# Reordering LayerNorm transposes, attention and the first stage in a two-layer transformer kernel

## The chip, the cores and the metric

The kernel runs on one core of one Trainium2 chip. The metric is device time in microseconds (us) for one execution; I quote the median of several runs. The kernel before takes 1357.69 us (median of 5 runs, 1355.87 to 1361.27).

Short names, as the profile has them: PE is TensorE (matmul), DVE is VectorE, ACT is ScalarE, POOL is GpSimd, SP is SyncE (here it only starts DMA transfers).

## The reference

Two layers. Each is a dilated sliding-window attention block followed by a feed-forward block, both with LayerNorm in front and a residual.

```python
# S=2048 rows, D=1024, H=32 heads of 32, window W=8 with dilation 2, F=3584; bf16
def A(x, wqkv, wo):                   # attention
    q, k, v = split(x @ wqkv)         # 1024 -> 3 * 1024
    logits = q . k[pos - 2*w] * 32**-0.5,  w = 0..7     # masked where pos < 2*w
    o = sum_w softmax(logits)[w] * v[pos - 2*w]
    return o @ wo
def B(x, w1, b1, w2, b2):             # feed-forward
    return gelu(x @ w1 + b1) @ w2 + b2
for layer in range(2):
    x = x + A(layernorm(x), wqkv, wo)
    x = x + B(layernorm(x), w1, b1, w2, b2)
```

## The kernel before

The 2048 rows are cut into four blocks of 512. Two layers of four blocks make eight **stages**, 0 to 7. The attention of a stage depends only on its own rows and a halo of 14 rows, so the stages are pipelined: while PE does the feed-forward block of stage n, it also projects Q, K, V for stage n+3, and DVE computes attention.

The framework places every instruction on its engine **in a fixed order at compile time**, from program order, priorities and a model of the times. In the traces each engine follows that order: DVE's evictions that were ready at 482.7 us start at 492.24 us, after the multiply that stands before them (shown below).

LayerNorm: arithmetic on DVE, the reciprocal root on POOL, then the transposes on PE, all for one tile of 128 rows at a time.

```python
def ln_T(xt, xnT, c):
    st = ...; nc.vector.bn_stats(...) x2; nc.vector.bn_aggr(mv, st)
    nc.vector.tensor_scalar(ve, mv[:, 1:2], EPS, None, ALU.add)
    nc.gpsimd.tensor_tensor(rs, ve, mhalf, ALU.pow)               # POOL: 1/sqrt
    nc.vector.tensor_scalar(xn, xt, mv[:, 0:1], rs, ALU.subtract, ALU.mult)
    for k in range(KT):                                           # 8 transposes on PE
        nc.tensor.transpose(pt[:, k, :], xn[:, k * P:(k + 1) * P], ident)
    nc.scalar.copy(xnT[:, :, c * P:(c + 1) * P], pt)
# LN1 (before the projections) and WO (before the feed-forward block) call ln_T for c = 0..3
```

Attention (about 81 us of DVE per stage) is traced with the lowest priority, right after its projections. Its largest steps are multiplies over 128 x 8192 elements.

```python
def ATT(l, j):
    # loads q, k, v from the scratch that QKV wrote
    with tc.high_priority(offset=-LOWP):
        # halos; per pair of window positions: pr = q * k (128 x 8192), three adds ("qk groups")
        # softmax; the exponential is on ACT
        # per pair: pr = v * aw (128 x 8192), adds into o ("value part")
    # stores o to scratch
```

Output projection and second feed-forward matmul. There are six PSUM accumulators for all matmuls; W2 holds four of them until DVE has added them to the residual ("eviction").

```python
def WO(l, j):
    # oT <- one load; two weight chunks
    for c in range(NC):
        for hf in range(2):
            # 8 matmuls into ps;  DVE: xr += ps
        ln_T(xr, xn2T, c)                 # LayerNorm 2 with its transposes, inside the loop
        nc.vector.tensor_tensor(xr, xr, b2bc, ALU.add)
def W2(l, j, hf):
    # 4 accumulators; weights in 4 groups of 7
    for g in range(4):
        for kk in range(7):
            for c in range(NC):
                nc.tensor.matmul(accs[c], ...)
    for c in range(NC):
        nc.vector.tensor_tensor(sl, accs[c], sl, ALU.add)
```

The order of the whole (shortened like the code above; the whole kernel follows):

```python
    LN1(0); QKV(0, mid=LN1(1)); att(0)    # "mid": LN1 of the next stage at weight chunk 2
    QKV(1, mid=LN1(2)); att(1)
    QKV(2, mid=LN1(3)); att(2)
    QKV(3, chunks 0..3); WO(0); QKV(3, chunks 4..5); att(3)
    for n in range(8):
        W1(n, mid=LN1(n + 3));            # n + 3 only where 1 <= n and n + 3 < 8
        QKV(n + 3); att(n + 3)
        W2(n, first half); WO(n + 1); W2(n, second half)
```

## Time and profile before

| | before |
|---|---|
| median of 5 runs | 1357.69 us |
| span of the profiled run | 1355.3 us |
| PE busy | 1272.8 us |
| matmuls / transposes on PE | 5632 / 512 |

The page's part on busy time (busy us, share of the span, number of instructions):

```profile
PE 1272.8 (94%) x6144; PEld 585.5 (43%) x6144; DVE 861.7 (64%) x831; ACT 352.8 (26%) x500; POOL 305.9 (23%) x346
```

PE is the engine that bounds the kernel, but a busy PE is not a fast PE. The timeline of PE (start us, duration us, engine, line, instruction, count; in brackets the idle time before it and what ended it) shows this in two places:

```profile
458.34 24.34 PE L316 MATMUL psw<-wchunk,h 128*128 128x512 bf16 x112
482.51 3.62 PE L275 MATMUL pswo<-wchunk,oT 128*128 128x512 bf16 x16
492.97 9.09 PE L275 MATMUL pswo<-wchunk,oT 128*128 128x512 bf16 x28 [6.84 <-DVE xr L322]
...
1139.71 48.51 PE L298 MATMUL psw<-xn2T,wchunk 128*128 128x512 bf16 x224
1188.06 24.34 PE L316 MATMUL psw<-wchunk,h 128*128 128x512 bf16 x112
```

From 1139.71 to 1188.06 us nothing waits: 224 matmuls in 48.35 us, 0.2159 us each. At 492.97 us PE has waited 6.84 us for an eviction, and the next 28 matmuls take 9.09 us where 28 x 0.2159 = 6.05 would do, so a wait costs more than its length: the granted clock is 0.50 from 492.97 to 497 us. DVE's timeline at the same moment says why the eviction was late:

```profile
487.89 4.42 DVE L223 TENSOR_TENSOR pr<-q,k 128x8192 bf16<-128x8192 bf16 x1
492.24 2.48 DVE L322 TENSOR_TENSOR xr<-psw,xr 128x512 bf16<-128x512 f32 x4
494.63 1.28 DVE L280 TENSOR_TENSOR xr<-pswo,xr 128x512 bf16<-128x512 f32 x2
```

W2's matmuls had been done by 482.7 us, but their four evictions (L322) stand in DVE's order behind attention, the last of it a 4.42 us multiply.

The waits of PE (in total us, times, longest us):

```profile
PE ptr L134 <- DVE xn L131: 26.7, 26, 6.2
PE pswo L275 <- DVE xr L322: 22.8, 5, 8.1
PE ptr L134 <- DVE ve L127: 12.6, 5, 6.7
PE ptr L134 <- POOL rs L129: 12.5, 1, 12.5
```

Three of the four are transposes (ptr) waiting for LayerNorm; the last one is the start.

The table of windows gives each stage (window in us; busy us of each engine; the granted PE clock; DMA share; GB/s):

```profile
core 0: us, PE busy (x) PEld busy (x) DVE busy (x) ACT busy (x) POOL busy (x), PEclk, DMA share, GB/s
356.48:533.17 176.69, 161.60 (x769) 73.84 (x768) 158.00 (x134) 45.61 (x64) 38.10 (x46) 0.95 0.70 214
698.98:862.27 163.29, 157.07 (x770) 71.75 (x769) 106.00 (x105) 44.94 (x63) 43.63 (x46) 1.00 0.69 213
1139.71:1253.16 113.45, 112.82 (x546) 51.61 (x545) 21.52 (x41) 23.30 (x32) 22.51 (x29) 1.00 0.50 167
```

The three rows are stages 1, 3 and 6 (a stage is counted from the first matmul of its W1). I call **loss** the length of a window minus 0.2159 us for each of its matmuls and 0.0556 us for each transpose (8 take about 0.45). Stages 1 and 3 hold the same work, 704 matmuls and 64 transposes, 155.5 us: they lose 21.2 and 7.8. Stage 6 loses 1.2. Over the whole span the work is 1244.1 us and the loss 111.2.

### The profile page before, as it was taken

The page shows a single profiled execution, that of the slowest core. Times are in us where ns is not written, and L with a number is a line of the kernel's source. Part 1 is how long each engine was busy: PE and PEld are TensorE (multiplying, and loading weights), DVE is VectorE, ACT ScalarE, POOL GpSimd, SP SyncE. Part 2 cuts the span into 40 slices and gives each one's busy share as a digit, 9 for nine tenths or more (in the row PEclk, how much of TensorE's full clock was granted, in tenths as well). Part 3 has the DMA queues.
Part 4 walks back from the last instruction along what each step waited for, and adds up shares of the span by engine and source line. Part 5 has one row for each costly group of instructions (what it writes and reads, how often), then busy time and mean ns, then how long its engine had stood idle before and what let it go on. Part 6 is the DMA issues. An engine that isn't in the chain of part 4 may idle for free.

```text
span 1355.3 us, 14546 instructions
## 1 busy us (share of the span) xinstructions
PE 1272.8 (94%) x6144; PEld 585.5 (43%) x6144; DVE 861.7 (64%) x831; ACT 352.8 (26%) x500; POOL 305.9 (23%) x346
## 2 busy tenths in 40 slices
PE   5899898997989979999899998999999999999998
PEld 3344344443444434444344444444444444444443
DVE  4379999999899989912999049970599451023001
ACT  2334223411234102432024311243113301401310
POOL 4312021111321212412133121322232122111110
PEclk9899899998989989999999999999999999999999
DMA  8665484773775947569575695756947437544542
GB/s 249 209 140 125 89 252 155 215 226 118 229 218 175 291 122 240 185 207 276 149 235 191 212 280 155 246 186 220 265 139 232 171 127 239 184 147 148 183 136 86
DMA packets 76866, 259.17 MB, mean 191 GB/s; under 512 B 8832, under 2 KB 17024, under 8 KB 74752
## 3 DMA queue, kind: packets, MB, share of 16 engines
q0 software_dynamic: 56352, 212.88, 49.6%
q1 hardware_dynamic: 16704, 45.09, 12.2%
q8 instruction: 48, 0.79, 0.3%
q10 hardware_dynamic: 3744, 0.27, 0.2%
q14 instruction: 18, 0.15, 0.0%
HBM read 216.28 MB, written 41.94 MB: 191 GB/s over the span
## 4 chain that ended last, share of the span: by engine, by line
PE 46%; DVE 35%; DMA 10%; issue 5%; POOL 4%; ACT 0%; SPq 0%; POOLq 0%; DVEq 0%
PE psw L298 18%; PE psqkv L171 12%; PE psw L316 12%; DVE pr L223 6%; DVE pr L247 4%; DVE pr L226 4%; DVE bnst L123 3%; POOL rs L129 3%; DMA k<-scrK 3%; PE pswo L275 2%; DVE pr L227 2%; DMA scrK<-stage 2%; DMA xin<-in_A_x_dram 2%; DMA v<-scrV 2%; DVE xn L131 2%
## 5 line engine op out<-in xcount | busy, mean ns | idle before, releaser
L298 PE MATMUL psw<-xn2T,wchunk 128*128 128x512 bf16 x1792 | 392.8, 381 | 0.7 <-DVE xr L322 0.7
L316 PE MATMUL psw<-wchunk,h 128*128 128x512 bf16 x1792 | 391.2, 379 | 0.0
L171 PE MATMUL psqkv<-xnT,wchunk 128*128 128x512 bf16 x1536 | 339.3, 383 | 1.1 <-ACT xnT L135 1.1
L298 PEld LDWEIGHTS <-wchunk 128*128 128x128 bf16 x1792 | 175.5, 98 | 210.6 <-issue 3.9
L316 PEld LDWEIGHTS <-h 128*128 128x128 bf16 x1792 | 174.8, 98 | 208.6
L171 PEld LDWEIGHTS <-wchunk 128*128 128x128 bf16 x1536 | 151.5, 99 | 183.7 <-issue 7.6
L303 ACT ACTIVATE h<-psw,b1raw 128x512 bf16<-128x512 f32 x224 | 154.0, 687 | 282.3 <-PE psw L298 282.2
L117 POOL DMA_DIRECT2D wchunk<-in_B_w_dram x120 | 114.6, 955 | 468.8 <-PE psw L316 208.8
L322 DVE TENSOR_TENSOR xr<-psw,xr 128x512 bf16<-128x512 f32 x64 | 39.5, 680 | 236.0 <-PE psw L316 236.0
L178 ACT CAST stage<-psqkv 128x512 bf16<-128x512 f32 x192 | 112.3, 586 | 210.1 <-PE psqkv L171 209.7
L275 PE MATMUL pswo<-wchunk,oT 128*128 128x512 bf16 x512 | 123.0, 396 | 22.8 <-DVE xr L322 22.8
L223 DVE TENSOR_TENSOR pr<-q,k 128x8192 bf16<-128x8192 bf16 x32 | 141.6, 4424 | 0.9
L247 DVE TENSOR_TENSOR pr<-v,aw 128x8192 bf16<-128x8192 bf16 x32 | 141.5, 4421 | 0.8
L210 DVE COPY k<-k 32x448 bf16<-32x448 bf16 x24 | 6.4, 268 | 183.0 <-DMA k<-scrK 182.7
L135 ACT COPY xn2T<-ptr 128x1024 bf16<-128x1024 bf16 x32 | 32.4, 1012 | 334.5 <-PE ptr L134 334.5
L129 POOL TENSOR_TENSOR rs<-ve,mhalf 128x1 f32<-128x1 f32 x64 | 62.3, 978 | 202.7 <-DVE ve L127 197.1
L134 PE MATMUL ptr<-ident,xn 128*128 128x128 bf16 x512 | 44.2, 240 | 52.7 <-DVE xn L131 26.7
L275 PEld LDWEIGHTS <-oT 128*128 128x128 bf16 x512 | 51.1, 101 | 85.4 <-issue 34.0
L226 DVE TENSOR_TENSOR pr<-pr 128x4096 bf16<-128x4096 bf16 x32 | 73.0, 2283 | 0.7
L134 PEld LDWEIGHTS <-xn 128*128 128x128 bf16 x512 | 34.9, 108 | 75.6 <-DVE xn L131 66.6
L123 DVE BATCH_NORM_STATS2 bnst<-xin 128x6 f32<-128x512 bf16 x64 | 41.2, 669 | 34.7 <-DMA xin<-in_A_x_dram 27.8
L117 POOL DMA_DIRECT2D wchunk<-in_A_wqkv_dram x30 | 26.9, 897 | 142.0 <-PE psw L298 93.6
(51 smaller groups left out, 608.5 us busy)
## 6 DMA issues: line engine op xcount, KB each, us to landing
wchunk<-in_B_w_dram POOLq DMA_DIRECT2D x56, 1024.0 KB, 6.3
wchunk<-in_B_w_dram POOLq DMA_DIRECT2D x64, 896.0 KB, 6.3
wchunk<-in_A_wqkv_dram POOLq DMA_DIRECT2D x30, 1024.0 KB, 6.3
wchunk<-in_A_wo_dram POOLq DMA_DIRECT2D x16, 1024.0 KB, 8.5
scrQ<-stage POOLq DMA_DIRECT2D x8, 1024.0 KB, 8.8
q<-scrQ SPq DMA_DIRECT2D x8, 1024.0 KB, 7.0
scrK<-stage POOLq DMA_DIRECT2D x8, 1024.0 KB, 8.9
k<-scrK SPq DMA_DIRECT2D x8, 1024.0 KB, 9.3
```

Source lines behind the costliest of these rows:

```text
L117: dma_w.dma_start(t[:, 0:nk, :], src)
L123: nc.vector.bn_stats(st[:, h, :], xt[:, h * 512:(h + 1) * 512])
L129: nc.gpsimd.tensor_tensor(rs[:], ve[:], mhalf[:], ALU.pow)
L171: nc.tensor.matmul(ps[:], wt[:, k, f4 * P:(f4 + 1) * P], xnT[:, k, :], start=(k == 0), stop=(k == KT - 1),)
L178: nc.scalar.copy(sg[:, :, t, :], ps[:].rearrange("p (c i) -> p c i", c=NC))
L223: nc.vector.tensor_tensor(pr[:], q[:].unsqueeze(1).to_broadcast([P, 2, DH, P]), win(k, 2 * g, 2), ALU.mult)
L226: nc.vector.tensor_tensor(pr[:, :, 0:16, :], pr[:, :, 0:16, :], pr[:, :, 16:32, :], ALU.add)
L247: nc.vector.tensor_tensor(pr[:], win(v, 2 * g, 2), aw[:, 2 * g:2 * g + 2, :].unsqueeze(2).to_broadcast([P, 2, DH, P]), ALU.mult,)
L275: nc.tensor.matmul(ps[:], oT[:, c * KT + t, :], wts[hf][:, t, :], start=(t == 0), stop=(t == KT - 1),)
L298: nc.tensor.matmul(ps[:], wt[:, k, f4 * P:(f4 + 1) * P], xn2T[:, k, :], start=(k == 0), stop=(k == KT - 1),)
L303: nc.scalar.activation(h[:], ps[:], ACTF.Gelu_apprx_tanh, bias=consts["b1T"][:, ft:ft + 1])
L316: nc.tensor.matmul(accs[c][:], hs[kt][:, c * P:(c + 1) * P], wt[:, kk, :], start=(kt == 0), stop=(kt == FT - 1),)
```

## The change

The intent: take every wait of PE out of the pipeline by choosing better places in the fixed orders. No matmul, no attention step and no byte is saved.

- LayerNorm is split: the arithmetic stays where it was, the transposes come two weight chunks later (about 14 us), or inside the second half of W2 for LayerNorm 2. `xn` gets four buffers.
- Attention of stages 4 to 7 is tied behind the last evictions of the running feed-forward block. A tie is an order on one engine, not a semaphore wait. Attention 1 is split around output projection 0, which moves earlier.
- The last weight group of W2 goes accumulator by accumulator, so that evictions can start earlier.
- The first stage loads x on two queues, its weights from SP instead of POOL, projects K before Q, and PE does 90 warm-up transposes while it waits. ACT's exponential is tied behind given evictions. The output projection's operand comes in four loads.
- Smaller moves: those four loads, K loaded before Q in attention, loads of the residual tied behind stores (`xanchor`), biases on SP.

```diff
+CH_ORDER = (2, 3, 0, 1, 4, 5)                      # weight chunks: K, Q, V
+    for i in range(90):
+        nc.tensor.transpose(warm[:, i % KT, :], ident[:], ident[:])  # warm-up
-    def ln_T(xt, xnT, c):
+    def ln_compute(xt):                             # without the transposes
+    def ln_transpose(key, cs):                      # the transposes and ACT's copy
@@ QKV
+                if exp_at is not None and pos * 4 + f4 == exp_at:
+                    after(state.pop("exp"), cp)
@@ ATT(l, j, anchor=None, split_g=None): anchored(...) on halos and qk multiplies;
@@ with split_g, the qk groups from split_g on and all the rest are returned as a function
@@ WO
-            dma_a.dma_start(oT[:], scrO[l][j * NC:(j + 1) * NC]...)
+            for c in range(NC):
+                dma_a.dma_start(oT[:], scrO[l][j * NC + c]...)
-            ln_T(xr, xn2T, c)
+            xns.append(ln_compute(xr))
@@ W2
+            order = [(kk, c) for kk in range(7) for c in range(NC)]
+            if g == 3:
+                order = [(kk, c) for c in range(NC) for kk in range(7)]
@@ order of the whole
+    def ln1_hooks(n, engs=None):
+        return {2: lambda: LN1a(*stages[n], engs=engs), 4: lambda: LN1b(*stages[n])}
+        LN1a(*stages[0], engs=[nc.sync, nc.scalar, nc.sync, nc.scalar])
...
+        att1_rest = ATT(*stages[1], split_g=2)
...
+        QKV(*stages[3], chunks=range(0, 3), wres=wres)
+        wo0_last = WO(*stages[0], ...)
+        att1_rest(wo0_last)
...
         for n in range(N):
-            QKV(*stages[nxt]); att(nxt)
+            QKV(*stages[nxt], exp_at=(17 if n == 1 else 5))
+            ATT_load(*stages[nxt])
         W2(*stages[n], 0)
+            hooks = {1: lambda: LN2b(*stages[n + 1], range(0, 2)),
+                     2: lambda: LN2b(*stages[n + 1], range(2, 4))}
+        last = W2(*stages[n], 1, ..., hooks=hooks)
+            ATT(*stages[nxt], anchor=last)
```

## The prediction

> **What bounds the kernel now.** TensorE: the table of busy time gives PE 1272.8 of 1355.3 us. Without waits (timeline of PE, 1139.71 to 1188.06 us) 224 matmuls take 48.35 us, 0.216 each; 8 transposes about 0.45. 5632 matmuls and 512 transposes at those rates are 1216 + 29 = 1245 us, so about 110 us is loss. By stages (table of windows): 17.6 us before the first projection matmul; 22 lost from 17.6 to 198 (projections); 17 to 356; 21 to 533; 10, 8 and 8 in the next three stages, to 1026; then about 1 per stage, and 5 at the end.
>
> The waits of PE name the causes: transposes waiting for LayerNorm (DVE xn 26.7 us, ve 12.6; POOL rs 12.5 is the start), and output-projection matmuls waiting for evictions by DVE (22.8 us, with evictions behind 4.42 us attention multiplies in the timeline). Most of the rest is clock: after such gaps matmuls run at half rate (at 492.97 us, 28 take 9.09 us instead of 6.05). The Trainium skill, "TensorE: Matmul & The Clock Gate", Part 1, says an idle window of about 3.4 us halves the clock; the granted clock here agrees.
>
> **What the change does.** PE's real work, DVE's attention work (about 81 us per stage) and bytes stay. It moves:
>
> 1. LayerNorm's transposes two weight chunks (about 14 us) behind its arithmetic. This should remove nearly all transpose waits, 39 us without the start, and the cold clock after them.
> 2. Attention of stages 4 to 7 behind the last evictions of a feed-forward block, under the next first-layer matmuls and projections (48 + 41 us, room for 81 + 9 us of DVE), out of the way of the output projection. The last weight group, ordered by accumulator, frees accumulators earlier. This removes most of the 22.8 us.
> 3. First stage: x on two queues, weights off POOL, K before Q. First matmul near 13 us.
> 4. Attention 1 split around output projection 0, which now comes at about 163 us instead of 198. Attention 0 can end near 157 us, and its result needs a store and a load (8.5 us until the load's issue here, and more). I expect a new PE wait of 5 to 10 us.
>
> It adds 90 warm-up transposes in the initial wait. They are doubtful: the same page, Part 4, says transpose mode does not count as busy for the clock. Here 64 matmuls took 15.6 us instead of 13.8 after 32 transposes: not settled, at most 2 us.
>
> **Sum.** 1245 of work + 12 start + 5 projections + 9 around output projection 0 and stage 0 + 4 (stage 1) + 6 (stages 2 to 4) + 4 end = 1285; I take 1280 us, range 1264 to 1305. Faster by over 2%: 0.97; within 2%: 0.025; slower by over 2%: 0.005.
>
> **What would show it.** PE's waits for xn and ve near zero after the start; on evictions under 6 us in all; stages 1 to 4 near 156 us each; attention of stages 4 to 7 under first-layer matmuls in DVE's timeline; one PE wait for attention output near 165 us.
>
> **What would make it wrong.** Engine orders that do not match real times: ScalarE's exponential waiting for DVE ahead of evictions, POOL's root behind a weight load, LayerNorm slowed by 4.4 us attention steps beyond 14 us. Faster stages also press DMA (0.9 to 1.0 busy in some 20 us windows): PE would wait for weights.

## The result, and the profile after

The kernel after takes **1277.0 us** (median of 8 runs, 1275.91 to 1280.02), beside 1358.93 us for the kernel before in the same rounds. The ratio is 0.9398, 95% interval 0.9382 to 0.9413. Ratios here and below are the mean time of one kernel's fast runs over that of the other's of the same rounds, so not quite the ratio of the medians quoted.

Busy time of the kernel after:

```profile
PE 1255.6 (99%) x6234; PEld 586.9 (46%) x6234; DVE 869.6 (68%) x831; ACT 352.3 (28%) x504; POOL 282.2 (22%) x340
```

PE is busy for 99% of a span that is 80.6 us shorter. Its busy time fell by 17 us although it does 90 more transposes: fewer matmuls run at half clock.

The waits of PE in the kernel after:

```profile
PE pswo L347 <- DVE xr L401: 3.9, 2, 2.1
PE psw L394 <- DVE xr L352: 3.1, 2, 2.1
PE ptr L163 <- DVE xn L152: 2.3, 3, 1.4
PE psw L373 <- DVE xr L401: 1.1, 1, 1.1
```

Outside the start, the transposes' waits on LayerNorm fell from 39.3 us to 0.2. At the start they fell from 12.5 us to 2.1, because the warm-up transposes fill most of that time. Waits on evictions fell from 23.5 us (0.7 of it in a line not shown above) to 8.1 (first, second and fourth line).

PE's timeline, first the start, then the output projection inside stage 2:

```profile
1.44 7.58 PE L83 MATMUL warm<-ident 128*128 128x128 bf16 x90 [1.44 <-POOL ident masks.py:199]
...
14.94 27.79 PE L205 MATMUL psqkv<-xnT,wchunk 128*128 128x512 bf16 x128 [1.23 <-ACT xnT L166]
...
593.98 13.98 PE L347 MATMUL pswo<-wchunk,oT 128*128 128x512 bf16 x64
607.79 6.21 PE L394 MATMUL psw<-wchunk,h 128*128 128x512 bf16 x28
613.83 1.06 PE L163 MATMUL ptr<-ident,xn 128*128 128x128 bf16 x16
614.73 6.21 PE L394 MATMUL psw<-wchunk,h 128*128 128x512 bf16 x28
```

In the same place of stage 2 the kernel before stopped PE for 3.01 us (at 660.60 us), and in stage 1 for the 6.84 us shown above. Now 64 matmuls run through, in stage 1 as well (from 438.11 us), and the transposes follow inside W2 without a bracket, that is, without a wait. DVE's timeline at the end of that W2:

```profile
629.42 0.69 DVE L401 TENSOR_TENSOR xr<-psw,xr 128x512 bf16<-128x512 f32 x1 [15.57 <-PE psw L394]
630.93 0.69 DVE L401 TENSOR_TENSOR xr<-psw,xr 128x512 bf16<-128x512 f32 x1 [0.82 <-PE psw L394]
...
633.95 0.69 DVE L401 TENSOR_TENSOR xr<-psw,xr 128x512 bf16<-128x512 f32 x1 [0.82 <-PE psw L394]
...
636.37 4.43 DVE L273 TENSOR_TENSOR pr<-q,k 128x8192 bf16<-128x8192 bf16 x1
```

DVE was idle for 15.57 us and waited for the accumulators, not the other way round; they come 1.5 us apart because the last group goes accumulator by accumulator; attention starts after them. The table of windows, stages 1 and 3 again:

```profile
320.75:477.90 157.15, 155.90 (x770) 72.44 (x769) 136.73 (x111) 44.19 (x63) 41.26 (x49) 1.00 0.80 241
633.75:789.60 155.85, 155.71 (x770) 72.44 (x768) 109.77 (x104) 44.19 (x63) 39.16 (x47) 1.00 0.71 223
```

Stage 3 went from 163.29 to 155.85 us with 155.5 us of work in it, and stage 1 from 176.69 to 157.15.

Losses of all profiled runs, worked out as above from the starts of the stages in PE's timeline. "Projections" runs from the first projection matmul to stage 0 and holds output projection 0. In the traces of e5 to e12 some 120 matmul records (2%) are missing, so I used the known number of matmuls of each stretch throughout.

| run | start | projections | stage 0 | stage 1 | stages 2-4 | stages 5-6 | stage 7 | sum |
|---|---|---|---|---|---|---|---|---|
| before | 15.9 | 29.2 | 10.6 | 21.2 | 26.6 | 2.3 | 5.4 | 111.2 |
| after | 13.1 | 1.5 | 5.4 | 1.6 | 1.5 | 3.5 | 4.1 | 30.7 |
| e1: after, transposes early | 13.1 | 14.1 | 8.8 | 13.3 | 15.9 | 7.7 | 4.1 | 77.0 |
| e2: after, attention early | 13.5 | 2.9 | 5.8 | 15.0 | 26.2 | 0.0 | 4.1 | 67.5 |
| e3: before, transposes late | 16.4 | 23.6 | 8.7 | 20.8 | 19.4 | 0.0 | 5.4 | 94.3 |
| e4: before, attention late | 15.7 | 28.8 | 11.8 | 11.5 | 15.1 | 7.6 | 5.4 | 95.9 |
| e5: no warm-up | 13.8 | 1.0 | 5.8 | 1.6 | 1.5 | 3.5 | 4.1 | 31.3 |
| e6: old start | 15.8 | 13.7 | 5.4 | 1.6 | 1.1 | 3.5 | 3.9 | 45.0 |
| e7: Q before K | 13.2 | 4.1 | 5.4 | 1.6 | 1.8 | 3.6 | 4.1 | 33.8 |
| e8: attention 1 whole | 13.4 | 14.1 | 14.9 | 0.4 | 1.1 | 3.5 | 4.1 | 51.5 |
| e9: old start, late exponential | 14.6 | 15.8 | 6.9 | 1.7 | 2.6 | 3.6 | 3.9 | 49.1 |
| e10: e2 without the root | 12.4 | 1.0 | 6.5 | 13.1 | 14.5 | 0.0 | 4.1 | 51.6 |
| e11: accumulators interleaved | 13.4 | 2.8 | 6.3 | 4.9 | 1.3 | 6.0 | 5.6 | 40.3 |
| e12: two more splits | 13.5 | 2.8 | 0.0 | 18.3 | 1.3 | 0.0 | 4.1 | 40.0 |

### The profile page after: what moved, and what is told of

It is laid out like the page before. It is cut to its first block, busy times and chain, and to the rows that moved or that the text cites. A ratio compares the mean times of both kernels' runs of the same rounds, so it can differ in the third digit from the quotient of the medians.

```text
span 1274.7 us, 14752 instructions
## 1 busy us (share of the span) xinstructions
PE 1255.6 (99%) x6234; PEld 586.9 (46%) x6234; DVE 869.6 (68%) x831; ACT 352.3 (28%) x504; POOL 282.2 (22%) x340
## 3 DMA queue, kind: packets, MB, share of 16 engines
q1 hardware_dynamic: 51360, 51.13, 14.9%
## 4 chain that ended last, share of the span: by engine, by line
PE 69%; DVE 22%; DMA 4%; issue 2%; ACT 1%; POOL 1%; POOLq 0%; ACTq 0%
PE psw L394 23%; PE psw L373 22%; PE psqkv L205 17%; PE pswo L347 6%; DVE pr L273 5%; DVE pr L311 3%; DVE pr L276 2%; DVE bnst L144 1%; DMA xin<-in_A_x_dram 1%; PE ptr L163 1%; DVE pr L277 1%; DMA wchunk<-in_A_wo_dram 1%; DVE pr L318 1%; DVE o L319 1%; DMA scrQ<-stage 1%
## 5 line engine op out<-in xcount | busy, mean ns | idle before, releaser
L373 PE MATMUL psw<-xnT,wchunk 128*128 128x512 bf16 x1792 | 390.2, 379 | 1.1 <-DVE xr L401 1.1
L205 PE MATMUL psqkv<-xnT,wchunk 128*128 128x512 bf16 x1536 | 334.6, 379 | 1.5 <-ACT xnT L166 1.2
L378 ACT ACTIVATE h<-psw,b1T 128x512 bf16<-128x512 f32 x224 | 153.2, 688 | 286.0 <-PE psw L373 286.0
L166 ACT COPY xnT<-ptr 128x1024 bf16<-128x1024 bf16 x64 | 60.8, 1024 | 353.5 <-PE ptr L163 353.5
L347 PE MATMUL pswo<-wchunk,oT 128*128 128x512 bf16 x512 | 112.3, 379 | 4.1 <-DVE xr L401 3.9
L150 POOL TENSOR_TENSOR rs<-ve,mhalf 128x1 f32<-128x1 f32 x64 | 45.6, 715 | 169.6 <-DVE ve L148 158.8
L276 DVE TENSOR_TENSOR pr<-pr 128x4096 bf16<-128x4096 bf16 x32 | 73.3, 2290 | 0.9
L144 DVE BATCH_NORM_STATS2 bnst<-xin 128x6 f32<-128x512 bf16 x64 | 41.5, 669 | 22.7 <-DMA xin<-in_A_x_dram 13.3
L319 DVE TENSOR_TENSOR o<-o,pr 128x4096 bf16<-128x4096 bf16 x24 | 54.9, 2289 | 0.6
L318 DVE TENSOR_TENSOR pr<-pr 128x4096 bf16<-128x4096 bf16 x24 | 54.9, 2288 | 0.7
L123 POOL DMA_DIRECT2D wchunk<-in_A_wqkv_dram x24 | 21.2, 883 | 145.8 <-PE psw L373 97.6
L352 DVE TENSOR_TENSOR xr<-pswo,xr 128x512 bf16<-128x512 f32 x64 | 43.2, 678 | 11.6 <-PE pswo L347 11.6
```

The lines of the kernel that those rows point to most:

```text
L123: (eng or dma_w).dma_start(t[:, 0:nk, :], src)
L205: state["mm"] = nc.tensor.matmul(ps[:], wt[:, k, f4 * P:(f4 + 1) * P], xnT[:, k, :], start=(k == 0), stop=(k == KT - 1),)
L276: nc.vector.tensor_tensor(pr[:, :, 0:16, :], pr[:, :, 0:16, :], pr[:, :, 16:32, :], ALU.add)
L318: nc.vector.tensor_tensor(pr[:, 0], pr[:, 0], pr[:, 1], ALU.add)
L319: nc.vector.tensor_tensor(o[:], o[:], pr[:, 0], ALU.add)
L347: nc.tensor.matmul(ps[:], oTs[c][:, t, :], wts[hf][:, t, :], start=(t == 0), stop=(t == KT - 1),)
```

## The experiments

### e1 to e4: are there two causes or one?

My theory had two kinds of wait that add: transposes waiting for LayerNorm, and matmuls waiting for evictions. The rival: one cause, a DVE crowded by attention, which makes both. Four kernels make a two by two: undo each part in the kernel after, do each part alone in the kernel before.

e1, in the kernel after:

```diff
-        return {2: lambda: LN1a(*stages[n], engs=engs), 4: lambda: LN1b(*stages[n])}
+        return {2: both}          # LN1a, then LN1b at once
 # in WO, for each c:
             xns.append(ln_compute(xr))
+            ln_transpose(("f", l, j), [c])
 # and the LN2b hooks in QKV(3) and in W2 taken out
```

> The kernel after, with the LayerNorm transposes issued right after their arithmetic again, for both norms; everything else kept. My theory (two separate kinds of wait, which add): the waits for xn and ve come back, and the cold clock after them, 40 to 50 us, so about 1317 to 1327 us. Rival theory (one cause, DVE crowded by attention; transposes waited only because of it): with attention already out of the way this costs under 15 us, so below 1292 us.

e2, in the kernel after:

```diff
-            QKV(*stages[nxt], exp_at=(17 if n == 1 else 5))
-            ATT_load(*stages[nxt])
+            QKV(*stages[nxt])
+            ATT_load(*stages[nxt]); ATT(*stages[nxt])
...
-            ATT(*stages[nxt], anchor=last)
```

e2 thereby drops the ties of ACT's exponential (`exp_at`) too, so it undoes a little more than the place of attention.

> The kernel after, with attention of stages 4 to 7 started again right after its projection, without the anchors; transposes stay late. My theory: waits of the output projection on evictions come back in stages 1 to 4, 15 to 25 us with the clock, so about 1292 to 1302 us; waits of transposes stay near zero. Rival (crowding is the one cause): about 40 us or more, above 1315 us, with waits of transposes too.

e3, in the kernel before:

```diff
-    xnp ... bufs=2
+    xnp ... bufs=4
-    def ln_T(xt, xnT, c):
+    def ln_compute(xt): ...      # and ln_transpose(key, cs), called at chunk 4 (LN1),
+                                 # at the last chunk of QKV(3), and at groups 1 and 2 of W2's second half
```

> The kernel before, with only the transposes moved late (four xn buffers, as the change has). My theory: 40 to 50 us gained, about 1308 to 1318 us, and evictions still waited for about 23 us. Rival (crowding): under 15 us gained, above 1343 us.

e4, in the kernel before:

```diff
-            QKV(*stages[nxt]); att(nxt)
+            QKV(*stages[nxt])
...
-        W2(*stages[n], 1, ...)
+        last = W2(*stages[n], 1, ...)
+        if nxt is not None:
+            ATT(*stages[nxt], anchor=last)
```

> The kernel before, with only attention of stages 4 to 7 moved behind the second-half evictions of the feed-forward block. My theory: 15 to 25 us gained, about 1333 to 1343 us, with transposes still waiting over 30 us. Rival (crowding): 40 us or more gained, below 1318 us, and transposes hardly waiting in stages 1 to 4.

Measured:

| | median us | ratio to before |
|---|---|---|
| before, same rounds | 1358.38 | 1 |
| e3: before, transposes late | 1338.06 | 0.9848 (0.9822 to 0.9873) |
| e4: before, attention late | 1341.38 | 0.9872 (0.9849 to 0.9895) |
| e2: after, attention early | 1313.14 | 0.9664 (0.9645 to 0.9684) |
| e1: after, transposes early | 1323.34 | 0.9739 (0.9711 to 0.9767) |

Neither theory holds as it was put. e1 and e4 came out where mine expected them; e2 and e3 fell between the two. For e1 that is in part luck: 12.6 of its 46 us are lost in the projections, where PE's one long wait, 7.71 us at 116.93 us, is for evictions that stand behind attention 0's exponential in ACT's order, and not for a transpose. Each part alone is worth about 20 and 17 us; undoing either costs 46 and 36. Stages 2 to 4 of the loss table show it best: 26.6 us before, 26.2 with late transposes but early attention (e2; 19.4 in the frame of the kernel before, e3), 15.9 with late attention but early transposes (e1; 15.1 in e4), 1.5 with both. The waits of PE in e2 say what late transposes waited for, although they now had 14 us of slack:

```profile
PE ptr L163 <- DVE xn L152: 17.3, 9, 4.1
PE psw L394 <- DVE xr L352: 6.7, 6, 2.1
PE pswo L347 <- DVE xr L401: 5.2, 2, 2.6
```

and in e1, with attention out of the way and no slack:

```profile
PE ptr L163 <- DVE xn L152: 33.4, 32, 4.6
```

So a third thing links the two: attention slows LayerNorm's arithmetic so much that it uses up the slack.

### e10: what slows LayerNorm

The timelines of DVE, POOL and PE in e2, in stage 3:

```profile
678.06 0.69 DVE L144 BATCH_NORM_STATS2 bnst<-xin 128x6 f32<-128x512 bf16 x1 [2.00 <-DMA xin<-xmid]
...
684.25 0.15 DVE L148 TENSOR_SCALAR ve<-mv 128x1 f32<-128x1 f32 x1
684.37 4.43 DVE L311 TENSOR_TENSOR pr<-v,aw 128x8192 bf16<-128x8192 bf16 x1
689.26 0.55 DVE L152 TENSOR_SCALAR xn<-xin,mv,rs 128x1024 bf16<-128x1024 bf16 x1 [0.47 <-POOL rs L150]
...
670.58 4.68 POOL L150 TENSOR_TENSOR rs<-ve,mhalf 128x1 f32<-128x1 f32 x1 [1.97 <-DVE ve L148]
675.13 0.59 POOL L175 DMA_DIRECT2D xin<-xmid  x1
...
684.55 4.68 POOL L150 TENSOR_TENSOR rs<-ve,mhalf 128x1 f32<-128x1 f32 x1 [4.13 <-DVE ve L148]
...
689.86 1.03 PE L163 MATMUL ptr<-ident,xn 128*128 128x128 bf16 x8 [3.77 <-DVE xn L152]
```

POOL's root, 128 x 1 elements, starts at 684.55 us and takes 4.68 us; the median of the run's 64 roots is 0.56. It ends 0.4 us after DVE's 4.43 us multiply. The Trainium skill, "SBUF — State Buffer", section "Who interferes with whom", says that DVE and GpSimd share a pair of SBUF ports under an exclusive lock, and that a DVE instruction with two SBUF inputs contends with a GpSimd instruction that reads SBUF. The multiply has two SBUF inputs, and this trace agrees: 4.68 us instead of 0.56. The experiment takes the root away and keeps the rest of e2. Its output is wrong, which doesn't matter for the time.

```diff
-        nc.gpsimd.tensor_tensor(rs[:], ve[:], mhalf[:], ALU.pow)
-        nc.vector.tensor_scalar(xn[:], xt[:], mv[:, 0:1], rs[:], ALU.subtract, ALU.mult)
+        nc.vector.tensor_scalar(xn[:], xt[:], mv[:, 0:1], ve[:], ALU.subtract, ALU.mult)
```

> The kernel of the run with early attention (1313.1 us), with POOL's power instruction taken out of LayerNorm; the result is wrong on purpose (rows scaled by the variance). In that run POOL's root took 4.68 us instead of 0.56 wherever DVE was in a 4.43 us attention multiply. If this lock-out is what makes late transposes wait again (17.3 us on xn, plus clock): the waits fall under 6 us, 1290 to 1300 us. Rival (attention steps ahead of xn in DVE's own order are enough): 1306 us or more, waits on xn above 10 us.

Measured: 1298.32 us, ratio 0.9564 (0.9542 to 0.9586), against 1313.14 us and 0.9664 for e2. The wait of the transposes fell from 17.3 us to 5.2:

```profile
PE pswo L345 <- DVE xr L399: 8.0, 3, 4.6
PE ptr L161 <- DVE xn L150: 5.2, 6, 1.1
```

The number came out as my theory had it, and stages 2 to 4 lose 14.5 us instead of 26.2. But the traces do not make the lock-out the main cause of the delay. In the lines of e2 above, the multiply (684.37 us) stands before `xn` in DVE's own order, so `xn` could not have started before it ended; DVE waited for the locked root for only 0.47 us. From the first statistics to the last `xn` of this LayerNorm, DVE's timeline gives:

| stage 3, LayerNorm 1 | in all | attention's steps among it |
|---|---|---|
| after | 12.1 us | 2.6 us |
| e2 | 27.0 us | 15.6 us |
| e10 | 24.3 us | 15.6 us |

So attention's steps, placed between those of LayerNorm in DVE's order, make most of the delay, as the rival had it. The root adds 2.7 us, mostly by a detour: POOL issues the load of the fourth x tile (675.13 us) only after a locked root, and DVE waits 2.00 us for it. This is enough to tip the balance: PE's wait in this place is 3.77 us in e2 and 1.07 in e10. What is left in e10 is mostly evictions behind attention. Limits of this test: without the root the framework also orders DVE anew, LayerNorm gets shorter everywhere (start and projections lose 3.0 us less), and there is no control with the root left out of the kernel after. How the whole gain of 15 us divides was therefore not shown.

### e11: the order of the last weight group

```diff
-            if g == 3:
-                order = [(kk, c) for c in range(NC) for kk in range(7)]
```

> The kernel after, with the last weight group of W2 interleaved over the four accumulators again. My theory: with DVE free of attention at that point, four evictions of 0.69 us in a row are hidden behind the first 16 output-projection matmuls (3.5 us), so only stage 0 and 5, where attention still runs, lose 1 to 3 us each, and the end loses about 1 us: 1278 to 1283 us. Rival (the order is a main part of the gain): 3 us or more per stage, above 1295 us.

Measured: 1286.33 us, ratio 0.9473 (0.9452 to 0.9495): 9 us slower than the kernel after, 3 more than I expected at most. The loss table shows where. Stages 2 to 4, where DVE is free when W2 ends, lose nothing (1.3 against 1.5). Stage 1 loses 3.3 us more, stages 5 and 6 2.5, stage 0 0.9, the end of stage 7 1.5; the projections, which have no W2 in them, lose 1.3 more for another reason (see e5). So the order pays exactly where attention still runs as W2 ends, and once at the very end.

### e5: the warm-up transposes

```diff
-    warm = psmm.tile([P, KT, P], BF16, tag="mm", name="warm")
-    for i in range(90):
-        nc.tensor.transpose(warm[:, i % KT, :], ident[:], ident[:])  # warm-up
```

> The kernel after, without the 90 warm-up transposes. They took 7.58 us, which fits about 50 at half rate and 40 at full rate, so my theory is now that transposes do release the clock; without them the 32 real transposes and the first 16 or more matmuls run at half rate, and the first 64 projection matmuls take about 15.6 us instead of 13.8. Time 1279 to 1281 us. Rival (transpose mode does not count for the clock, as the skill's page says): no change, 1276 to 1278 us.

Measured: 1278.24 us, ratio 0.9408 (0.9389 to 0.9428). The interval overlaps that of the kernel after (0.9382 to 0.9413): no difference shown, so the time falls between my theory and the rival. The timeline of PE shows that the rival's reason was nevertheless wrong:

```profile
10.41 1.89 PE L160 MATMUL ptr<-ident,xn 128*128 128x128 bf16 x16 [10.41 <-DVE xn L149]
12.55 1.55 PE L160 MATMUL ptr<-ident,xn 128*128 128x128 bf16 x16 [0.25 <-ACT xnT L163]
15.57 27.79 PE L202 MATMUL psqkv<-xnT,wchunk 128*128 128x512 bf16 x125 [1.48 <-ACT xnT L163]
```

The first 16 transposes take 1.89 us, half rate; the next 16 speed up to 1.55; the matmuls that follow run at full rate from the first. Only transposes had run by then, so transposes do release the clock. My expectation that the first matmuls would be slow was wrong for the same reason: here the 32 real transposes warmed PE up by themselves. They did so in e4 too (second 16 in 1.52 us), but not in the kernel before and in e3 (1.93 us). Nor do warm-up transposes make it sure: in e2, e9, e11 and e12 they were there, and the second 16 real transposes still ran at half rate (1.92 to 1.93 us). In e11 and e12 the first 125 or so projection matmuls then took about 29.6 us instead of 27.8, which covers the 1.3 us that their projections lose more.

### e6 and e9: the start

e6, in the kernel after:

```diff
-        LN1a(*stages[0], engs=[nc.sync, nc.scalar, nc.sync, nc.scalar])
+        LN1a(*stages[0], engs=[nc.sync] * NC)
-                        pool=(None if pos < 4 else pools["wextra"]), eng=nc.sync,
+                        pool=(None if pos < 4 else pools["wextra"]),       # weights from POOL
```

> The kernel after, with stage 0's x on one queue and the projection weights on POOL again. My theory: first projection matmul near 17 us instead of 14.9, and nothing more, because the late transposes of stage 1 have slack: 1279 to 1281 us. Rival (the queues are a main part of the gain in the projections): 10 us or more, with PE waiting for stage 1's LayerNorm, above 1286 us.

Measured: 1290.83 us, ratio 0.95 (0.948 to 0.952), 14 us slower; my theory said 2 to 4. The first projection matmul came at 17.64 us as expected, which is 2.7 us. The rest is not LayerNorm of stage 1 either, as the rival had it. The timelines of ACT and PE:

```profile
118.75 1.06 ACT L301 ACTIVATE lg<-lg 128x1024 f32<-128x1024 f32 x1 [16.95 <-DVE lg L300]
...
120.33 24.77 PE L205 MATMUL psqkv<-xnT,wchunk 128*128 128x512 bf16 x102 [8.79 <-ACT stage L212]
```

The exponential of attention 0 stands at a fixed place among ACT's evictions. DVE was late with the logits, ACT sat 16.95 us, no projection was evicted, the six accumulators filled, and PE stopped for 8.79 us. In the kernel after the same ACT wait is 8.46 us and costs PE 0.3: just inside the slack. I took the fixed place of the exponential for the cause and moved it 12 evictions later:

```diff
-        QKV(*stages[2], wres=wres, hooks=ln1_hooks(3))
+        QKV(*stages[2], wres=wres, hooks=ln1_hooks(3), exp_at=8)
```

> The kernel of the run with the old start (1290.8 us; there ScalarE sat 16.95 us in its fixed order at attention 0's exponential, and PE waited 8.8 us for the evictions behind it), with that exponential moved 12 evictions later in ScalarE's order and nothing else. If the fixed place of the exponential is what made the old start cost 14 us: PE's wait on the stage copies vanishes, about 1279 to 1283 us. Rival (late loads themselves, or DMA contention, cost it): 1288 us or more.

Measured: 1295.61 us, ratio 0.9543 (0.9521 to 0.9564). My theory fell as it was put. PE's wait on the stage copies did vanish, but another took its place:

```profile
PE pswo L347 <- DMA oT<-scrO: 11.2, 1, 11.2
```

Output projection 0 now waits for the result of attention 0. So attention 0 runs late in both runs, and in e6 the exponential was only the first place where PE felt it. Part of the lateness in e9 is the edit's own: DVE waits 4.49 us for the moved exponential (0.82 in e6), so attention 0 starts 2.0 us earlier than in e6 and ends 2.7 us later. A smaller shift was not tried, and it might have cost less. DVE's timeline gives its first multiply and its last add:

| | first multiply of attention 0 | last add ends | operand loads issued from |
|---|---|---|---|
| before | 75.55 | 165.39 | 173.98 |
| after | 60.83 | 145.32 | 150.45 |
| e7: Q before K | 63.68 | 149.11 | 158.40 |
| e6: old start | 71.96 | 158.10 | 163.16 |
| e9: old start, late exponential | 69.98 | 160.81 | 170.43 |

Why it starts 11 us later in e6 than in the kernel after I can follow only in part: POOL issues the store of K at 41.59 us instead of 36.14, because in its order the roots of stage 2's LayerNorm come first and wait for x; and K is loaded by 65.08 us instead of 51.72, also because the load itself takes 14.9 us instead of 7.4. Which of the two queue changes is responsible was not separated.

### e7: K before Q

```diff
-CH_ORDER = (2, 3, 0, 1, 4, 5)
+CH_ORDER = (0, 1, 2, 3, 4, 5)
```

> The kernel after, with the projections in the order Q, K, V again. Attention 0 should start about 3 us later (K needs the longer load), and output projection 0, at 166.5 us, has more slack than that: my theory is no change, 1276 to 1279 us. Rival (the predicted wait of the output projection for attention was avoided only by K coming first): PE waits 3 us or more there and the time is 1281 us or more.

Measured: 1279.26 us, ratio 0.942 (0.9395 to 0.9445); its interval overlaps that of the kernel after; the time is 0.3 us above my range and below the rival's. Attention 0 started 2.9 us later, as expected, and PE did wait a little for it, which I had not expected:

```profile
PE pswo L347 <- DMA oT<-scrO: 1.8, 1, 1.8
```

The operand loads were issued 8.0 us later than in the kernel after, and 1.8 us of that reached PE. So the kernel after has about 6 us of slack there (an estimate from these two numbers).

### e8: attention 1 in one piece

```diff
-        att1_rest = ATT(*stages[1], split_g=2)
+        ATT(*stages[1])
...
-        att1_rest(wo0_last)
```

> The kernel after, with attention 1 not split around output projection 0. My theory: evictions of output projection 0 and of the feed-forward block queue behind 4.4 us steps of attention; PE waits 4 to 8 us there, 1281 to 1286 us. Rival (no need for the split, six accumulators cover it): 1276 to 1279 us.

Measured: 1298.36 us, ratio 0.9549 (0.9528 to 0.9571), 21 us slower, where I expected 4 to 8. The mechanism was right, the size was not, because it strikes more than once: the waits of PE name an eviction of output projection 0, and one of the next stage.

```profile
PE pswo L347 <- DVE xr L401: 7.1, 3, 5.1
PE pswo L347 <- DVE xr L352: 4.9, 1, 4.9
```

Projections lose 14.1 us instead of 1.5 and stage 0 14.9 instead of 5.4. About two fifths of these losses are no wait (17.2 of 29.0 us are) but mostly, as before, slower matmuls after one.

### e12: a candidate for a better version

The kernel after still loses 5.4 us in stage 0 and 3.5 in stage 5, both by evictions behind attention (attention 2 and attention 7). The candidate splits these as the change splits attention 1.

```diff
-        ATT_load(*stages[2]); ATT(*stages[2])
+        ATT_load(*stages[2]); att_rest[0] = ATT(*stages[2], split_g=2)
...
+            if n in att_rest:
+                att_rest.pop(n)(wo_last)              # behind output projection n + 1
+            if n == 0:
+                ATT_load(*stages[3]); ATT(*stages[3])
...
-            QKV(*stages[nxt], exp_at=(17 if n == 1 else 5))
+            QKV(*stages[nxt], exp_at=(21 if n == 1 else 5))
-            ATT(*stages[nxt], anchor=last)
+            r = ATT(*stages[nxt], anchor=last, split_g=(4 if nxt == N - 1 else None))
+            if r is not None: att_rest[n + 1] = r
```

> A candidate meant to beat both kernels: the kernel after, with attention 2 split around output projection 1 and the value part of attention 7 held behind output projection 6, as the change does for attention 1; attention 3's exponential four evictions later. The losses left in stages 0 and 5 (5.4 and 3.5 us, evictions behind attention multiplies) should shrink to about 1 us together: 1269 to 1273 us. If the fixed order goes wrong in stage 1, where attention 3 now runs later: 1277 us or more.

Measured: 1284.42 us, ratio 0.9458 (0.9436 to 0.948), slower than the kernel after. Both halves of the expectation came true at once. Stages 0 and 5 lose 0.0 us; but stage 1 loses 18.3 instead of 1.6. The timelines of DVE and PE there:

```profile
442.27 4.43 DVE L311 TENSOR_TENSOR pr<-v,aw 128x8192 bf16<-128x8192 bf16 x1
446.62 1.88 DVE L401 TENSOR_TENSOR xr<-psw,xr 128x512 bf16<-128x512 f32 x3
...
447.35 12.99 PE L347 MATMUL pswo<-wchunk,oT 128*128 128x512 bf16 x47 [5.43 <-DVE xr L401]
```

Attention 3, pushed back by the split of attention 2, now reaches into output projection 2. The split of attention 7 acts only in stage 5; by this profile it would be worth 3.5 us over the kernel after (an estimate, about 1273 us). It was not run by itself.

## Why the prediction was right

I predicted 1280 us, 1264 to 1305; the kernel takes 1277.0. Term by term, against the losses of the profiled run:

| term | predicted | measured |
|---|---|---|
| work of PE | 1245 | 1244.1 |
| start | 12 | 13.1 |
| projections | 5 | 1.5 |
| wait at output projection 0, and stage 0 | 9 | no wait at output projection 0, 5.4 in stage 0 |
| stage 1 | 4 | 1.6 |
| stages 2 to 4 | 6 | 1.5 |
| stages 5 and 6 | none | 3.5 |
| end | 4 | 4.1 |

- **The method held.** Splitting the loss by stage, and asking of each stage which wait ends, gave a sum within 11 us of the span (1285 against 1274.7). I then took 5 us off by judgement, which happened to be in the right direction.
- **Transposes.** The 39 us of waits went, with the cold clock after them, as predicted. Shown by e1: putting them back brings 33.4 us of these waits and costs 46 us, though 12.6 of the 46 are in the projections, where the long wait is another one (see e1).
- **Evictions.** I wrote "under 6 us in all"; it is 8.1. I had not counted that attention 7 would run into output projection 6 (stage 5, 3.5 us): stage 5 has no projections in it, so DVE has only W1 and half of W2, 48.4 + 24.2 us, for 81 us of attention.
- **The sum over parts was a coincidence of one kind.** I treated the two main parts as adding. e1 to e4 and e10 show that they do not: late transposes give slack, and only late attention lets LayerNorm fit into it, because attention's steps stand between LayerNorm's on DVE; the lock on POOL's root adds to it. My list of what could go wrong named the main mechanism (LayerNorm slowed by 4.4 us attention steps beyond 14 us) but not the lock, and the sum did not use it. The total came out right because both parts were there.
- **Output projection 0.** The predicted new wait of 5 to 10 us did not come. The step that was off: "Attention 0 can end near 157 us". It ended at 145.32. It started at 60.83 and took 84.5 us. The text gives no start and no length for it. By my working, it would start about there, with some 18 us of LayerNorm of the next two stages in between; but their statistics ran before attention 0 began (from 28.4 and 55.3 us), when DVE had nothing else to do. The dependence is real: with attention 0 ending 15.5 us later in e9, PE waits 11.2 us exactly there (some 3.7 of the 15.5 are due to the moved exponential).
- **Start.** The first matmul came at 14.94 us, not near 13. I gave the queues of the first stage little weight beyond that. e6 shows that they are worth 14 us, not 3, because attention 0 starts 11 us earlier with them.
- **Warm-up.** "At most 2 us hang on it": e5 shows no difference. My doubt about transposes and the clock was unfounded; in e5 the benefit is small because the real transposes did the same.

## What to carry to other kernels

In a program with fixed engine orders, moving a consumer later is worth only as much as the producer can use of the slack; look at what else runs on the producer's engines in that time, and try the two moves together and apart. A wait that disappears may turn up at the next consumer of the same late result (e6 and e9), so look for the first late event and not for the place where PE stops. After a wait the clock costs extra, so count losses against the undisturbed rate and not by idle time alone.

## What the Trainium skill lacked or had wrong

- "TensorE: Matmul & The Clock Gate", Part 4, says that transpose mode does not count as busy for the clock gate. Here 90 transposes, with no other matmul before them, start 106 ns apart at first and 56 ns apart from 5.1 us on (starts in the trace of the kernel after), and in e5 transposes alone brought PE to the full rate (16 in 1.89 us, the next 16 in 1.55, then matmuls at full rate from the first).
- The same page, Part 1, puts the release at about 3.4 us of activity. In the ten runs with warm-up transposes that step came 3.7 (e9) to 5.9 us (e6) after the first of them. Each of the ten came later than 3.4 us.
- "SBUF — State Buffer", section "Who interferes with whom", agrees with these runs. No page that I used says what follows for LayerNorm: a 128 x 1 instruction on POOL takes 4.68 us instead of 0.56 when DVE is in a two-input multiply of 4.43 us. DVE lost only 0.47 us by it directly, and 2.00 us by a load that POOL issued after such a root (e2, stage 3).
